# Two more blocks' first product, and block 0's second product, by seven products in a fused retention-and-GELU kernel

## The chip, the cores and the metric

The program runs on one core of one Trainium2 chip. The time is device microseconds of that core, the median of several executions; lower is better. The profile's own "span" (first to last instruction) is about 2 us shorter than the time. All executions quoted here are of the fast state. Ratios are the mean time of one kernel's fast runs over the mean time of the other's fast runs of the same rounds on the same chip, so they are not quite the ratios of the medians that stand beside them.

Engines: PE multiplies matrices and writes the results to a memory called PSUM, which is used in banks; DVE and ACT do element work and empty PSUM; POOL issues most loads here; SP issues stores and DMA transposes. PEld in the profile is PE's loading of the operand that stays in the array during a matmul.

## The reference, cut to what matters

```python
# q, k, v: (8 batches, 8 heads, 576 tokens, 64)
scores = (1/sqrt(64)) * q @ k^T
ret    = scores * where(i >= j, gamma[h] ** (i - j), 0)
x      = (ret @ v), heads side by side            # 4608 x 512
h      = x @ w_in                                 # 512 x 2048
out    = gelu_exact(h) @ w_out                    # 2048 x 512
```

The attention part is done in chunks of 128 tokens (the last of a batch has 64), 40 chunks in all. A chunk's q and k have to be transposed first ("turned" below), on PE or by DMA. The second part is done in 9 blocks of 512 tokens, numbered 0 to 8. Each block has a **first product** (x with w_in, then GELU) and a **second product** (GELU's result g with w_out).

## The kernel before

The program text does not contain a schedule. A builder writes it: it keeps a clock of its own (`clock[0]`), estimates when each operand will be ready, and at each turn emits the next step whose estimate says "ready".

Blocks 1 to 8 already compute the second product by seven products of quarter matrices instead of eight (the Strassen-Winograd scheme): 112 matmuls of 256 columns instead of 64 of 512. `left` is a quarter of g or a sum S1 to S4 of quarters, `right` a quarter of w_out (B) or a sum T1 to T4. Block 0 computes it plainly, in `mlp2_step`.

```python
def mlp_ready(step):                          # "2": block 0, plain
    ...
    if kind == "s":
        return fast_ready(t, step[2])
    ts, m0, m1 = step[2:]
    when = max(land_out[(m1 - 1) // 2],       # <- when this piece of w_out lands
               g_ready(t, ts * 128, ts * 128 + 128, range(m0, m1)))
    ...

def fast_ready(t, n):                         # "s": blocks 1 to 8, seven products
    k, p = (LAST_ORDER if t == N_BLK - 1 else FAST_ORDER)[n]
    lhs, rhs, where = PRODUCTS[k]
    if lhs[0] == "S":
        when = max(s_end.get((t, q_, int(lhs[1])), 1e6) for q_ in range(N_DF // 4))
    else:
        ...
        when = g_ready(t, lo, lo + 128, range(int(lhs[2]) - 1, N_DF, 2))
    ...                                       # accumulators, a free PSUM bank
    if rhs[0] == "T":
        when = max(when, w_sum_end[0])
    return when                               # nothing here asks when w_out ("B") lands
```

## Time and profile before

| | before |
|---|---|
| time | 298.81 us (298.47 to 299.09, 4 runs) |
| span | 296.9 us |
| first `hT` matmul / last matmul starts | 12.5 / 293.1 us |
| PE, DVE, ACT busy | 97%, 57%, 44% |
| granted PE clock | 0.998 |

From the page of the kernel before: the span, the busy time of the engines, and two rows of the span in 40 slices (7.4 us each): busy tenths of PE and granted PE clock in tenths.

```profile
span 296.9 us, 7431 instructions
...
PE 288.6 (97%) x3151; PEld 192.8 (65%) x3151; DVE 169.1 (57%) x368; ACT 130.9 (44%) x259; POOL 113.8 (38%) x146
...
PE   6999999999999999999999999999999999999995
...
PEclk9999999999999999999999999999999999999999
```

PE is full from the second slice on. The clock row has a 9 everywhere, but its record only begins at 15.9 us: matmuls of 128 columns start 107 ns apart at 12.7 us and 55 ns apart at 16.1 us, so the early ones ran at half clock. From 16 us on the clock is full. PE's chain of waits (shares of the span by engine, then by line) also shows PE as the limit:

```profile
PE 84%; DMA 7%; DVE 6%; POOL 2%; issue 1%; POOLq 0%; DVEq 0%
PE hT L403 38%; PE fast L535 32%; DMA v_ld<-in_v_dram 4%; PE sc L295 3%; PE o_ps L331 3%; PE o_ps L370 2%; PE oT L435 2%; PE u_ps L351 2%; DMA w_in<-in_moe_w_in_dram 2%; DMA qk_ld<-in_q_dram 1%; PE qk_ps L270 1%; DVE vh L316 1%; POOL qk_ld L185 1%; DVE s L468 1%; DVE qkT L273 1%
```

`hT` is the first product, `fast` the second by seven products, `oT` the plain one of block 0. Pieces of that chain in order of time (start us, duration us, what):

```profile
113.21 0.24 PE u_ps L351 x8
...
118.01 0.12 PE u_ps L351 x8
...
267.34 13.81 PE hT L403 x64
281.15 12.24 PE fast L535 x112
```

A plain first product of a block lasts 13.81 us, a second product by seven 12.24 us. A group of eight `u_ps` matmuls lasts 0.12 us behind another of its shape and 0.24 us behind another shape, so a change of shape costs about 0.12 us.

### The profile page before, as it was taken

What the parts mean: (1) busy time and instruction counts of PE and PEld (TensorE: products, weight loads), DVE (VectorE), ACT (ScalarE), POOL (GpSimd) and SP (SyncE); (2) the same over time, 40 slices, a digit from 0 to 9 for tenths busy, and PEclk for the clock granted to TensorE, in tenths of its full rate; (3) what the DMA queues carried; (4) which work ended last, traced back from release to release, by engine and by line L of the source; (5) the groups of instructions that cost most, each with busy time, mean ns of one, the idle gap of its engine ahead of it and who ended that gap; (6) DMA issues with size and microseconds to landing.
All of it is one profiled execution on the core that took longest, in us unless ns stands there. A gap on an engine that the chain in (4) does not pass through costs nothing.

```text
span 296.9 us, 7431 instructions
## 1 busy us (share of the span) xinstructions
PE 288.6 (97%) x3151; PEld 192.8 (65%) x3151; DVE 169.1 (57%) x368; ACT 130.9 (44%) x259; POOL 113.8 (38%) x146
## 2 busy tenths in 40 slices
PE   6999999999999999999999999999999999999995
PEld 2675755658865488557864786568656864784584
DVE  4652646947779726986089827581775144402422
ACT  4676502655235613554246414651465146426621
POOL 8997879838485260690781075000000000000000
PEclk9999999999999999999999999999999999999999
DMA  9999999999999999999999999900300030003013
GB/s 92 152 182 176 190 187 187 199 144 131 155 147 202 166 155 149 210 157 166 77 230 137 134 78 223 162 10 3 141 2 2 0 143 0 2 5 137 3 35 106
DMA packets 153089, 35.48 MB, mean 119 GB/s; under 512 B 141792, under 2 KB 148960, under 8 KB 153056
## 3 DMA queue, kind: packets, MB, share of 16 engines
q0 software_dynamic: 117872, 18.23, 86.4%
q1 hardware_dynamic: 35184, 16.78, 31.9%
q8 instruction: 24, 0.39, 0.5%
q14 instruction: 9, 0.07, 0.1%
HBM read 36.70 MB, written 9.44 MB: 155 GB/s over the span
## 4 chain that ended last, share of the span: by engine, by line
PE 84%; DMA 7%; DVE 6%; POOL 2%; issue 1%; POOLq 0%; DVEq 0%
PE hT L403 38%; PE fast L535 32%; DMA v_ld<-in_v_dram 4%; PE sc L295 3%; PE o_ps L331 3%; PE o_ps L370 2%; PE oT L435 2%; PE u_ps L351 2%; DMA w_in<-in_moe_w_in_dram 2%; DMA qk_ld<-in_q_dram 1%; PE qk_ps L270 1%; DVE vh L316 1%; POOL qk_ld L185 1%; DVE s L468 1%; DVE qkT L273 1%
## 5 line engine op out<-in xcount | busy, mean ns | idle before, releaser
L403 PE MATMUL hT<-xT,w_in 128*128 128x512 bf16 (+7 forms) x692 | 130.2, 345 | 1.0 <-DVE xT L382 0.8
L409 ACT ACTIVATE g<-hT 128x512 bf16<-128x512 f32 (+6 forms) x173 | 89.5, 527 | 53.7 <-PE hT L403 50.9
L403 PEld LDWEIGHTS <-w_in 128*128 128x128 bf16 x692 | 62.0, 98 | 59.5 <-issue 0.9
L535 PEld LDWEIGHTS <-s 128*128 128x128 bf16 x512 | 49.6, 98 | 7.0 <-DVE s L468 0.8
L185 POOL DMA_DIRECT2D qk_ld<-in_q_dram x39 | 33.9, 869 | 47.1 <-DMA qkT<-qk_ld 39.9
L306 DVE TENSOR_TENSOR ret<-sc,msk 128x512 bf16<-128x512 f32 x64 | 41.1, 682 | 11.1 <-PE sc L295 10.7
L535 PE MATMUL fast<-w_sum,s 128*128 128x256 bf16 x384 | 43.8, 273 | 0.5 <-DVE s L468 0.5
L535 PEld LDWEIGHTS <-g 128*128 128x128 bf16 x384 | 37.5, 98 | 5.8
L185 POOL DMA_DIRECT2D v_ld<-in_v_dram x39 | 34.0, 871 | 12.9 <-DVE s L468 3.5
L559 DVE TENSOR_TENSOR o_sb<-fast,u 128x512 f32<-128x512 f32 (+1 forms) x18 | 11.4, 631 | 48.2 <-PE fast L535 39.2
L185 POOL DMA_DIRECT2D qk_ld<-in_k_dram x39 | 33.9, 869 | 5.6 <-DMA v_ld<-in_v_dram 4.4
L535 PE MATMUL fast<-w_out,g 128*128 128x256 bf16 x256 | 29.3, 273 | 0.0
L382 DVE TENSOR_TENSOR xT<-o_ps,dq 128x512 bf16<-128x512 f32 (+1 forms) x42 | 24.3, 605 | 7.4 <-PE o_ps L370 5.8
L467 DVE TENSOR_TENSOR s<-g 128x512 bf16<-128x512 bf16 x32 | 13.4, 420 | 25.0 <-ACT g L409 24.8
L555 ACT COPY u<-fast 128x512 f32<-128x512 f32 (+1 forms) x18 | 9.7, 538 | 39.9 <-PE fast L535 39.9
L356 ACT CAST u_sb<-u_ps 128x256 bf16<-128x256 f32 x32 | 11.9, 372 | 32.2 <-PE u_ps L351 32.1
L316 DVE TENSOR_TENSOR vh<-v_ld,dv 128x512 bf16<-128x512 bf16 x32 | 21.2, 680 | 6.4 <-DMA v_ld<-in_v_dram 6.4
L535 PE MATMUL fast<-w_out,s 128*128 128x256 bf16 x128 | 15.6, 272 | 0.0
L535 PE MATMUL fast<-w_sum,g 128*128 128x256 bf16 x128 | 15.3, 273 | 0.0
L435 PE MATMUL oT<-w_out,g 128*128 128x512 bf16 x64 | 15.2, 380 | 0.0
L295 PE MATMUL sc<-qkT 64*64 64x128 bf16 (+1 forms) x576 | 14.1, 223 | 0.5 <-ACT qkT L276 0.4
L468 DVE TENSOR_TENSOR s<-s,g 128x512 bf16<-128x512 bf16 x32 | 13.6, 425 | 1.1
(62 smaller groups left out, 192.6 us busy)
## 6 DMA issues: line engine op xcount, KB each, us to landing
out_dram<-o_sb SPq DMA_DIRECT2D x14, 512.0 KB, 4.7
qk_ld<-in_k_dram POOLq DMA_DIRECT2D x32, 128.0 KB, 7.3
v_ld<-in_v_dram POOLq DMA_DIRECT2D x32, 128.0 KB, 7.4
qk_ld<-in_q_dram POOLq DMA_DIRECT2D x31, 128.0 KB, 7.3
w_in<-in_moe_w_in_dram POOLq DMA_DIRECT2D x8, 256.0 KB, 6.8
w_out<-in_moe_w_out_dram POOLq DMA_DIRECT2D x8, 256.0 KB, 7.8
out_dram<-o_sb SPq DMA_DIRECT2D x4, 256.0 KB, 5.8
out_dram<-o_sb SPq DMA_DIRECT2D x8, 128.0 KB, 1.7
```

The lines of the kernel that those rows point to most:

```text
L185: nc.gpsimd.dma_start(dst[:cs], src[b, :, c0:c0 + cs, :].rearrange("h s d -> s h d"))
L295: nc.tensor.matmul(sc[e][lo:lo + 64, hp, :cs], lhsT=qkT[sl, 1, hp, lo:lo + 64], rhs=qkT[sl, 0, hp, :cs], start=True, stop=True, skip_group ...
L306: nc.vector.tensor_tensor(r[:cs, :, :cs], sc[e][:cs, :, :cs], msk[:cs, :, :cs].to_broadcast([cs, HP, cs]), op=ALU.mult)
L316: nc.vector.tensor_tensor(vh[:cs], loaded[i][1][:cs], dv[:cs, :, ci:ci + 1].to_broadcast([cs, H, D]), op=ALU.mult)
L356: nc.scalar.copy(u, u_ps[0])
L382: nc.vector.tensor_tensor(xT[:, :, at:at + hi - lo], s["o_ps"][:, :, lo:hi], dq[:, :, c0 + lo:c0 + hi], op=ALU.mult)
L403: nc.tensor.matmul(hT[:, :hi - lo], lhsT=w[:, cc, o:o + 128], rhs=xT[:, cc, tok0 % RING + lo:tok0 % RING + hi], start=(cc == 0), stop=(cc ...
L409: nc.scalar.activation(g_of(t, m, lo, hi), hT[:, :hi - lo], AF.Gelu)
L435: nc.tensor.matmul(oT, lhsT=g_of(t, m, ts * 128, (ts + 1) * 128), rhs=w_out_sb[:, m // 2, m % 2, :], start=(m == 0), stop=(m == N_DF - 1))
L467: nc.vector.tensor_tensor(u[:, 0], a[2, 1], a[2, 2], op=ALU.add)
L468: nc.vector.tensor_tensor(u[:, 1], u[:, 0], a[1, 1], op=ALU.subtract)
L535: nc.tensor.matmul(acc_[:, p, :], lhsT=left(t, lhs, j, p), rhs=right(rhs, j), start=(fresh and j == 0 and (p == 0 or apart)), stop=(j == N ...
```

## The change

Its intent: (1) the first product of blocks 7 and 8 also by seven products ("lean"), woven into the second product of the block in front; (2) the second product of block 0 by seven products as well, so that `mlp2_step` goes; (3) the running state sum kept in SBUF instead of in a PSUM bank of its own; (4) attention groups by a list instead of by a rule; (5) another order of the first loads and a finer estimate of DMA times in the builder. The diff, cut to its core:

```diff
-    N_PE_TR = 10
+    N_PE_TR = 9
+    N_DYN = 3
+    N_LEAN = 7
+    LOADS = "1 2 3 i i i 4 i o i i 5 i i 6 o 7 o 8 o o o o o"   # chunks, w_in, w_out
+    PLAN = [(1, 16), (1, 5), (1, 110), (0, 103), ... ]              # 34 groups: chunks, not before
-    FAST_FROM = 1
+    FAST_FROM = 0
...
-    for what in "1 i 2 i i 3 z i i i i i 4 5 o o o o 6 o o o o 7 8".split():
+    for what in LOADS.split():
...
-    def mlp2_step(t, ts, m0, m1):
-        wait(land_out[(m1 - 1) // 2])
-        ...
+    def states(upto):                      # two chunks' states in one bank
+        ...                                # run_sum (SBUF) += u_ps on DVE, u = run_sum on ACT
+    def lean_step(t, n, x):
+        ...                                # 7 products, 4 matmuls of 256 columns each
+        if k == 1: keep("m1")
+        elif k == 2: add("c11", "m1", acc_)
+        ...                                # then GELU from SBUF
...
+    stages = [first_runs[0], first_runs[1] + [second_run[0]], ...]
+        if t + 1 >= N_LEAN and t + 1 < N_BLK:
+            stages.append(lean_runs + [second_run[t]] if LEAN_FIRST else ...)
...
-        if kind == "s":
-            return fast_ready(t, step[2])
-        ts, m0, m1 = step[2:]
-        when = max(land_out[(m1 - 1) // 2], g_ready(t, ts * 128, ts * 128 + 128, range(m0, m1)))
-        return max(when, free_at[first_free()[0]]) if m0 == 0 else when
+        if kind == "f":
+            return lean_ready(*step[1:])
+        return fast_ready(t, step[2])
```

## The prediction

> What bounds the kernel now. The page gives PE 97% busy, DVE 57%, ACT 44%. The chain of waits is 84% PE; from 12.5 us, where the first hT matmul starts, to the last matmul at 293.1 us it is almost only PE. The PE waits list barely 3 us, most of it before 12.5 us. So the span is 12.5 us of start, 280.6 us of PE instructions back to back, and 3.8 us of tail. In the timeline the first product of a late block (64 matmuls of 512 columns) lasts 13.81 us (216 ns each); the second by seven products (112 of 256) lasts 12.23 us (109 ns each). Block 0's second product is still plain: 64 oT matmuls, 13.8 us.
>
> What the change does to PE.
> 1. Blocks 7 and 8: first product by seven products, 4 x 7 x 4 = 112 matmuls of 256 columns: 12.23 instead of 13.81 us, -1.6 us each, -3.2 us.
> 2. Block 0's second product by seven products too (the threshold goes from 1 to 0): -1.6 us.
> 3. Nine instead of ten chunks turned on PE: -0.45 us.
> 4. Listed groups and states of two chunks in one bank. A u_ps group takes 0.12 us behind another of its tile shape and 0.24 us behind another shape (chain): a change of shape costs about 0.12 us. The Trainium skill ("TensorEngine Tiling (Array Packing)", Key Properties) says that changing the mode drains the engine; the trace agrees. I count 107 changes now, and expect 95 to 100 after: -1 us.
> 5. Loads reordered: chunks 1 to 3 ahead of the first w_in piece. The first hT slips from 12.5 to about 16 to 18 us, but then runs 512 wide with more attention behind it; I book 0, with +-2 us. Early matmuls run at 107 ns per 128 columns until 16 us, as the skill's "TensorE: Matmul & The Clock Gate" (Part 1) has it for a cold array; that stays.
> Sum: about -6.3 us.
>
> What it adds elsewhere. DVE: 32 state sums (about 0.4 us each, 13 us), 24 adds of the lean products (0.69 us), about half of 24 copies, sums of w_in (32) and x (8), 16 sums of block 0: 169 to about 220 us. ACT stays near 130 to 140 us. In a woven stage (12.2 + 12.2 us of PE) I count about 21 us of DVE: tight, but two open chains and the second product as filler should cover waits of 0.9 us. The sums of block 8's g can only begin when block 7's use of the sum buffers ends; 16 sums of about 0.35 us against about 5.3 us of PE work that needs none: perhaps 0.3 us of stall. I book +0.5 us for this.
>
> Predicted: 292.5 us, range 289.0 to 296.0; faster by over 2% (below 293.03) 0.57, within 2% 0.41, slower 0.02.
>
> Right or wrong would show as: 224 lean matmuls at 109 ns; hT 512-wide count down by 128; no oT; PE still the chain to the end; two woven stages of about 24.5 us; last stage still about 12.2 us and tail 3.8 us; DVE 215 to 225 us; attention finished some 40 us earlier than the 242 us of now; the first hT later.
>
> What would make it wrong: PE waiting on DVE s, m1/u2/u4 or lean sums in the woven stages (then 294 to 297); early starvation, because all w_out and their sums must land before block 0's second product, while transposes share the DMA (slower); or the listed order removing hidden start stalls, worth 2 to 3 us more than I book (then 289 to 290).

## More of the kernel before

The order in which steps are emitted is the order in each engine's queue. Semaphores keep the result right whatever the order; the estimates decide only the order.

```python
while True:                                   # the builder's loop
    picks = attention_picks()                 # attention, sums, turns of chunks
    due = [p for p in picks if p[0] <= clock[0] + SOON]
    if due: attend(*due[0][1:]); continue
    pick = mlp_pick()                         # a step of a first or second product
    if pick is not None and pick[0] <= clock[0] + SOON:
        mlp(pick[1]); continue
    ...                                       # else move the clock on
```

How block 0 got over the time in which w_out was still landing is to be seen in PE's timeline (start, duration, instruction; no bracket at the end means no idle time before it) and in one stretch of time (its bounds, its length, PE busy, PEld, DVE, ACT, POOL busy, each with its count, then granted clock as a share of full clock, DMA busy share, GB/s):

```profile
35.48 3.63 PE L435 MATMUL oT<-w_out,g 128*128 128x512 bf16 x16
...
52.04 1.04 PE L435 MATMUL oT<-w_out,g 128*128 128x512 bf16 x4
```

```profile
36.00:49.00 13.00, 13.00 (x122) 6.46 (x120) 5.23 (x11) 2.05 (x5) 9.81 (x12) 1.00 1.94 175
```

The plain `oT` takes w_out two rows of tiles at a time, from 35.5 us on, as its pieces land; PE is busy 13.00 of 13.00 us between 36 and 49 us.

## The result, and the profile after

306.50 us (305.60 to 306.76, 4 runs) against 298.81 us; the ratio is 1.0253, 95% interval 1.0227 to 1.0278. The change made the kernel 2.5% slower. Forecast were 292.5 us and at most 296.0.

The page after, same lines as before:

```profile
span 303.9 us, 7902 instructions
...
PE 282.8 (93%) x3304; PEld 209.5 (69%) x3322; DVE 216.6 (71%) x492; ACT 137.2 (45%) x274; POOL 112.5 (37%) x143
...
PE   6889716999999999999999999999999999999995
...
PEclk9999955999999999999999999999999999999999
```

PE's busy time is 5.8 us less than before (288.6 to 282.8), yet the span is 7 us longer. In slices 5 to 7 (30 to 53 us) PE's row has a hole, 7 1 6, and in slices 6 and 7 the granted clock is 5 tenths. The chain of waits has lost PE's share and gained DMA's, with a new name in it:

```profile
PE 80%; DMA 10%; POOL 5%; DVE 2%; issue 1%; POOLq 0%; DVEq 0%
PE fast L573 36%; PE hT L469 28%; PE lean L706 7%; DMA w_out<-in_moe_w_out_dram 5%; DMA w_in<-in_moe_w_in_dram 5%; PE sc L330 3%; PE o_ps L366 2%; POOL qk_ld L224 2%; PE o_ps L422 2%; PE u_ps L389 2%; POOL v_ld L224 1%; POOL w_in L235 1%; DVE u L721 1%; DVE ret L341 0%; POOL qk_ld L113 0%
```

The waits of PE (engine, line, releaser: total us, times, longest us), the new one and that of the lean products:

```profile
PE fast L573 <- DMA w_out<-in_moe_w_out_dram: 10.6, 6, 3.6
...
PE lean L706 <- DVE u L721: 0.5, 1, 0.5
```

PE's timeline at that place (the bracket is idle time before the instruction and its releaser):

```profile
35.06 1.03 PE L469 MATMUL hT<-xT,w_in 128*128 128x512 bf16 x4
35.93 0.44 PE L573 MATMUL fast<-w_out,g 128*128 128x256 bf16 x2
39.93 0.37 PE L573 MATMUL fast<-w_out,g 128*128 128x256 bf16 x1 [3.56 <-DMA w_out<-in_moe_w_out_dram]
43.76 0.37 PE L573 MATMUL fast<-w_out,g 128*128 128x256 bf16 x1 [3.45 <-DMA w_out<-in_moe_w_out_dram]
...
48.88 0.37 PE L573 MATMUL fast<-w_out,g 128*128 128x256 bf16 x1 [0.90 <-DMA w_out<-in_moe_w_out_dram]
49.05 3.41 PE L469 MATMUL hT<-xT,w_in 128*128 128x192 bf16 x20
...
52.84 1.15 PE L469 MATMUL hT<-xT,w_in 128*128 128x192 bf16 x12
```

This is one step, the first of block 0's second product: eight matmuls, one for each piece of w_out. It was emitted at 35.93 us, right behind the last matmul of block 0's first product, and its last matmul started at 48.88 us, when the last piece had landed. Nothing else ran on PE in those 13 us, although 20 matmuls of 192 columns of block 1 stood behind it. The Trainium skill ("PSUM — Partial Sum Buffer", Engine vs sequencer instructions) says that matmuls start and complete in program order; the trace agrees. That stretch, to be held against the one of before, and the next 11 us:

```profile
36.00:49.00 13.00, 2.36 (x9) 0.75 (x8) 3.15 (x8) 0.85 (x2) 9.56 (x13) 0.61 1.72 184
49.00:60.00 11.00, 11.00 (x141) 10.29 (x140) 5.45 (x11) 6.27 (x18) 9.93 (x12) 0.84 2.38 158
```

PE was busy for 2.36 of 13.00 us, and the granted clock fell to 0.61; it was 0.84 in the stretch after. The skill ("TensorE: Matmul & The Clock Gate", Part 1) says that the array's clock falls to half after an idle window of about 3.4 us and needs about as long at work to come back. The trace agrees on the way back: the clock record is full again at 52.5 us, 3.5 us after the work resumed; the twenty matmuls of 192 columns from 49.05 us start 160 ns apart, those from 52.84 us 82 ns apart. On the way down less idle time was enough: the clock fell at 38.9 us, and in the 3.4 us before that PE had been busy for 0.89 us, so idle for 2.5.

```profile
35.48:38.89 3.41, 0.89 (x5) 0.39 (x4) 3.38 (x10) 0.90 (x2) 3.08 (x5) 1.00 2.02 170
38.89:42.31 3.42, 0.37 (x1) 0.10 (x1) 0.29 (x1) 0.00 (x0) 2.39 (x5) 0.50 2.04 172
```

Why it was emitted there: after the change block 0 goes through `fast_ready`, and that asks for g, for sums and for a bank, but not for w_out. For blocks 1 to 8 that had never mattered, because w_out lands once and was there long before. The line that asked, `land_out[...]`, stood in the branch that the change took out. The builder, run once more with a print in it, shows the moment: at 35.07 us of its clock block 1's next piece of x was estimated 0.4 us away, this step was "ready", and so it was put in front. The builder's own estimate for the last piece of w_out was 48.7 us, within 0.2 us of the truth; nobody asked for it. By its clock this order even ends 0.6 us earlier (286.7 us) than the mended one of e1 (287.3 us), so the builder could not have warned.

To see where time went over the whole run I summed, over each trace, the times from the start of one PE matmul to the start of the next, by the kind of the first (us; a wait is counted with the matmul before it):

| kind | before | after | e1 (below) | e9 (below) |
|---|---|---|---|---|
| first products (`hT`, `lean`) | 127.0 | 125.6 | 124.9 | 122.8 |
| second products (`fast`, `oT`) | 113.8 | 123.4 | 112.6 | 111.1 |
| attention (`sc`, `o_ps`, `u_ps`) | 37.8 | 36.3 | 36.4 | 34.6 |
| turns of chunks (`qk_ps`) | 6.1 | 5.8 | 5.4 | 7.6 |
| dummy matmuls and the rest at the start | 7.2 | 8.2 | 8.6 | 7.5 |
| sum | 291.9 | 299.3 | 287.9 | 283.6 |

The second product should have lost 1.6 us and gained 9.6; everything else stands near or below where it stood.

### The profile page after: what moved, and what is told of

It reads as the page before. It is cut to its first block, busy times and chain, and to the rows that moved or that the text cites. A ratio compares the mean times of both kernels' runs of the same rounds, so it can differ in the third digit from the quotient of the medians.

```text
span 303.9 us, 7902 instructions
## 1 busy us (share of the span) xinstructions
PE 282.8 (93%) x3304; PEld 209.5 (69%) x3322; DVE 216.6 (71%) x492; ACT 137.2 (45%) x274; POOL 112.5 (37%) x143
## 4 chain that ended last, share of the span: by engine, by line
PE 80%; DMA 10%; POOL 5%; DVE 2%; issue 1%; POOLq 0%; DVEq 0%
PE fast L573 36%; PE hT L469 28%; PE lean L706 7%; DMA w_out<-in_moe_w_out_dram 5%; DMA w_in<-in_moe_w_in_dram 5%; PE sc L330 3%; PE o_ps L366 2%; POOL qk_ld L224 2%; PE o_ps L422 2%; PE u_ps L389 2%; POOL v_ld L224 1%; POOL w_in L235 1%; DVE u L721 1%; DVE ret L341 0%; POOL qk_ld L113 0%
## 5 line engine op out<-in xcount | busy, mean ns | idle before, releaser
L469 PE MATMUL hT<-xT,w_in 128*128 128x512 bf16 (+6 forms) x576 | 102.1, 330 | 2.1 <-DMA w_in<-in_moe_w_in_dram 1.0
L473 ACT ACTIVATE g<-hT 128x512 bf16<-128x512 f32 (+6 forms) x148 | 71.6, 494 | 65.6 <-PE hT L469 64.1
L469 PEld LDWEIGHTS <-w_in 128*128 128x128 bf16 x592 | 53.9, 100 | 43.9 <-DMA w_in<-in_moe_w_in_dram 1.4
L573 PEld LDWEIGHTS <-s 128*128 128x128 bf16 x576 | 55.8, 98 | 6.9
L573 PEld LDWEIGHTS <-g 128*128 128x128 bf16 x432 | 41.8, 98 | 16.9 <-issue 11.0
L573 PE MATMUL fast<-w_sum,s 128*128 128x256 bf16 x432 | 49.8, 273 | 0.0
L573 PE MATMUL fast<-w_out,g 128*128 128x256 bf16 x288 | 35.4, 275 | 10.6 <-DMA w_out<-in_moe_w_out_dram 10.6
L505 DVE TENSOR_TENSOR s<-g 128x512 bf16<-128x512 bf16 x36 | 15.1, 419 | 12.6 <-ACT g L473 11.6
L404 ACT CAST u_sb<-run_sum 128x256 bf16<-128x256 f32 x24 | 9.7, 405 | 21.3 <-DVE run_sum L401 14.9
L308 DVE COPY qkT<-qk_ps 128x512 bf16<-128x512 bf16 (+1 forms) x12 | 4.3, 396 | 19.2 <-PE qk_ps L305 19.2
L507 DVE TENSOR_TENSOR s<-g 128x512 bf16<-128x512 bf16 x36 | 15.0, 418 | 0.0
## 6 DMA issues: line engine op xcount, KB each, us to landing
qk_ld<-in_k_dram POOLq DMA_DIRECT2D x32, 128.0 KB, 7.0
v_ld<-in_v_dram POOLq DMA_DIRECT2D x32, 128.0 KB, 7.1
qk_ld<-in_q_dram POOLq DMA_DIRECT2D x31, 128.0 KB, 7.2
out_dram<-o_sb SPq DMA_DIRECT2D x8, 128.0 KB, 1.7
```

The lines of the kernel that those rows point to most:

```text
L469: nc.tensor.matmul(hT[:, :hi - lo], lhsT=w[:, cc, o:o + 128], rhs=xT[:, cc, tok0 % RING + lo:tok0 % RING + hi], start=(cc == 0), stop=(cc ...
L473: nc.scalar.activation(g_of(t, m, lo, hi), hT[:, :hi - lo], AF.Gelu)
L505: nc.vector.tensor_tensor(u[:, 0], a[2, 1], a[2, 2], op=ALU.add)
L507: nc.vector.tensor_tensor(u[:, 2], a[1, 1], a[2, 1], op=ALU.subtract)
L573: nc.tensor.matmul(acc_[:, p, :], lhsT=left(t, lhs, j, p), rhs=right(rhs, j), start=(fresh and j == 0 and (p == 0 or apart)), stop=(j == N ...
```

## The experiments

Theory A: the one step emitted 13 us too early caused the loss, by holding PE and then by the cold clock; the rest of the change works. Rival B: w_out lands late because the DMA queues are full, and PE starves then in whatever order. Rival C: the woven stages and the added DVE work (216.6 against 169.1 us busy) cost the time. All kernels gave correct results. The times of e1, e2, e3, e6, e7 and e10 fell where theory A or the prediction's view put them; those of e4, e8, e9 and e11 missed their forecasts, as told below.

### e1: only the readiness rule mended

```diff
+        if rhs[0] == "B":
+            when = max(when, max(land_out))
         if rhs[0] == "T":
             when = max([when] + list(w_sum_end.values()))
```

> The changed kernel with one thing mended: the readiness rule of the second product also waits for all w_out pieces, so block 0's first step is listed after block 1's first matmuls instead of at 35.9 us. Theory A (one step of 8 matmuls, placed in PE's queue 13 us before its operands land, held up all that stood behind it): the waits of fast on w_out (10.6 us) go and so does the cold array after them; 306.5 falls to 294 to 297. Rival B (w_out lands late because the DMA queues are full, so PE starves then whatever the order): 302 or more. Rival C (the woven stages or the extra DVE work cost the time): 304 to 306.

Measured: 294.46 us (294.24 to 295.80) against 298.83 us of before on that chip, ratio 0.986 (0.981 to 0.991): clear of noise. Against the 306.50 us of the changed kernel two lines give back 12.0 us. (The changed kernel ran in another call; the kernel before has the same median in both, 298.81 and 298.83 us, so the medians may be compared.) Slices, timeline and stretches of e1, as shown of the others:

```profile
PE   6979999999989999999999999999999999999995
...
PEclk9999999999999999999999999999999999999999
```

```profile
37.02 2.15 PE L469 MATMUL hT<-xT,w_in 128*128 128x192 bf16 x24 [0.43 <-DVE xT L434]
...
56.26 3.66 PE L575 MATMUL fast<-w_out,g 128*128 128x256 bf16 x32
```

```profile
36.00:49.00 13.00, 11.88 (x221) 10.27 (x220) 12.71 (x28) 7.88 (x23) 9.54 (x13) 1.00 1.71 184
49.00:60.00 11.00, 11.00 (x99) 8.82 (x98) 6.88 (x11) 7.00 (x18) 9.34 (x12) 1.00 2.48 157
```

The step now starts at 56.26 us behind block 1's first product, the clock stays at 1.00, and the waits of `fast` on w_out are gone from the list. The DMA queues are as busy as in the changed kernel in that stretch (184 GB/s in both), so rival B falls: PE had other work, and the order kept it from it.

### e2 and e3: without the lean first products, with and without the mend

```diff
-    N_LEAN = 7
+    N_LEAN = 9
```

> The changed kernel with the early stall kept, but blocks 7 and 8 computed with the plain first product (the threshold raised to 9). Theory A: the lean products are worth their matmul saving of 3.2 us, so this runs at about 309 to 310. Rival C: they cost time, so this runs below 306.

> Both edits: the mended readiness rule and no lean first products. Theory A: the two effects add, so about 3 us above e1_landing. Rival C: at or below e1_landing.

Measured: e2 309.44 us (308.68 to 309.90), 2.9 us above the changed kernel; e3 298.10 us (296.14 to 298.66), 3.6 us above e1, both on the chip of e1. The lean products are worth what their matmuls save (3.2 us was forecast), stall or no stall. Rival C falls. The chain of e1 shows that the woven stages have no hole worth naming:

```profile
227.53 1.75 PE lean L708 x16
...
269.26 20.18 PE fast L575 x184
289.47 0.42 DVE o_sb L599
```

From 227.53 us to the last element work at 289.47 us PE does five things of 12.23 us each (two lean first products, the second products of blocks 6, 7 and 8), 61.2 us in 61.9 us. DVE's extra work is off the path there. e3 is also the change without its main idea, and it is no faster than the kernel before (0.9955, 0.990 to 1.001): what else it brought came to nearly nothing.

### e4: the stall kept, but the array kept at work

```diff
         for j in range(N_DF // 2):
+            if t == 0 and n == 0:
+                warm((0, 0, 14, 14, 4, 4, 4, 4)[j])      # dummy matmuls of 512 columns
             nc.tensor.matmul(acc_[:, p, :], ...)
```

> The changed kernel, stall kept, but dummy matmuls put between the eight waiting matmuls of the step, fewer than fit the waits, so that the array has work while it waits. It splits theory A's loss in stall and cold clock after it. The hT matmuls of 192 columns just behind the stall took about 160 ns instead of 83 ns, some 6 us at half rate: 2.5 to 3.5 us should be won, 303 to 304. If the clock plays no part: 306.5, the same.

Measured: 304.35 us (304.23 to 305.10), 2.2 us below the changed kernel, somewhat less than forecast. So of the 12.0 us that e1 gives back, about 2.2 us were the cold clock after the stall and the remaining 9.9 us or so the stall itself (306.50 - 304.35, and 304.35 - 294.46). The forecast took 6 us at half rate; the trace of the changed kernel has 3.5 us of work at half rate (49.05 to 52.54 us), half of which, 1.75 us, is an estimate of the same loss. The split is good to about half a microsecond. Part of the timeline, and the stretch:

```profile
41.03 0.27 PE L575 MATMUL fast<-w_out,g 128*128 128x256 bf16 x1
41.25 3.18 PE L891 MATMUL warm<-zeros 128*128 128x512 bf16 x14
44.27 0.27 PE L575 MATMUL fast<-w_out,g 128*128 128x256 bf16 x1
...
49.46 1.81 PE L469 MATMUL hT<-xT,w_in 128*128 128x192 bf16 x20
```

```profile
36.00:49.00 13.00, 12.77 (x79) 6.22 (x80) 4.98 (x13) 1.50 (x3) 9.54 (x13) 1.00 1.72 184
```

The matmuls of 192 columns behind the stall now start 82 ns apart from the first on (20 in 1.65 us). The stretch is also a warning. The skill's "Perfetto Trace Analysis" (Identifying the Most-Contended Engine) calls matmul busy time a bad measure of how close a kernel is to its limit, because matmuls are pipelined; here it misleads for another reason: PE is busy 12.77 of 13.00 us, 10.4 us of it with dummies. A gap can be hidden from the busy share as well as filled.

### e6: e1 with block 0's second product plain again

`mlp2_step` and its readiness rule put back for block 0 (`FAST_FROM = 1`), all else as in e1.

> e1_landing with block 0's second product plain again, as in the kernel before (64 matmuls of 512 columns that take the w_out pieces two by two as they land), all else as in e1_landing. Prediction's view: the seven products are worth 1.6 us there, so 296.0. Rival: at that time DVE and DMA set the pace (16 sums of g are 5.9 us of DVE between 28 and 37 us, and every w_out piece must have landed), so the saving is lost: within 0.5 us of e1_landing (294.5) or below it.

Measured: 296.13 us (295.71 to 299.88) against 299.50 us of before on that chip, ratio 0.992 (0.982 to 1.002); e1 had 0.986 on another chip. The difference of the ratios, 0.006, is 1.8 us (one of e6's four runs, 299.88 us, raises its mean); by medians, each against its own before, it is 1.0 us; between the profiled spans it is 1.5 us (294.0 and 292.5). PE's time on second products, summed as in the table above, is 114.1 us in e6 and 112.6 us in e1, also 1.5 us. The intervals overlap, so the size is uncertain, but 1.0 to 1.8 us fits the forecast 1.6 us and speaks against the rival that DVE and DMA eat the saving.

### e7: rule as it was, w_out loaded earlier

```diff
-    LOADS = "1 2 3 i i i 4 i o i i 5 i i 6 o 7 o 8 o o o o o"
+    LOADS = "1 2 3 i i i 4 i i i i i 5 o o o o o o o o 6 7 8"
```

> The changed kernel with its readiness rule as it was, and only the order of the first loads changed: all w_in pieces, chunk 5, all eight w_out pieces, then chunks 6 to 8. The early step stays early (the kernel's own bookkeeping places it at 33 us), but its operands should land at about 42 us instead of 48.9. Theory A: the waits of fast on w_out shrink from 10.6 us to 5 to 8 us; but x of block 1 comes later, so PE has less to do after it, and little of that is won in the total: 302 to 307. If the place of the step were not the cause but the lateness of w_out alone, it should come near e1_landing (294.5).

Measured: 306.24 us (305.05 to 307.47) against 299.82 us of before on that chip, ratio 1.022 (1.018 to 1.026); the changed kernel has 1.025. The waits on w_out halved, and others came in their place:

```profile
PE fast L573 <- DMA w_out<-in_moe_w_out_dram: 5.1, 6, 1.0
PE o_ps L366 <- DVE ret L341: 2.7, 6, 0.7
...
PE fast L573 <- DVE w_sum L490: 0.9, 1, 0.9
```

The step stalled less, but chunks 6 to 8 now came behind w_out, and PE waited for attention's operands (`ret`) more than before, 2.7 us against 0.7; that the order of the chunks is the reason was not tested. The clock took a part too. It fell at 39.2 us although no wait on w_out was longer than 1.02 us; PE had been busy for 0.81 of the 3.4 us before:

```profile
35.75:39.17 3.42, 0.81 (x3) 0.29 (x3) 3.26 (x10) 0.00 (x0) 2.21 (x4) 1.00 1.24 205
39.17:42.58 3.41, 1.68 (x8) 1.02 (x8) 0.00 (x0) 0.00 (x0) 2.45 (x4) 0.50 2.10 166
```

After the stall PE worked for about 7.4 us at half clock (41.3 to 46.0 and 50.1 to 52.8 us), against 3.5 us in the changed kernel; half of the difference, 2 us, is an estimate of what that cost more. Moving data to suit a wrong order did not help; moving the instruction did.

### e8, e9, e10, e11: new lists under the mended rule

`LOADS` and `PLAN` look like the result of a search by the builder's clock, which then held the faulty rule. I searched both lists anew by random changes under the mended rule, by the builder's own clock, and ran two results. Against e1 only the two lists differ; e9's are:

```diff
-    LOADS = "1 2 3 i i i 4 i o i i 5 i i 6 o 7 o 8 o o o o o"
+    LOADS = "i 1 2 3 i i 4 i 5 i 6 i i i 7 8 o o o o o o o o"
-    PLAN = [(1, 16), (1, 5), (1, 110), (0, 103), ... ]
+    PLAN = [(1, 136), (0, 119), (1, 187), (0, 100), (1, 94), (1, 22), (1, 0), (0, 184), (2, 175), (0, 103), (1, 9),
+            (1, 0), (0, 14), (2, 24), (1, 51), (2, 61), (2, 15), (1, 16), (2, 0), (2, 15), (2, 31), (2, 20), (2, 0),
+            (2, 3), (2, 96), (2, 102), (2, 47), (2, 174), (1, 30), (2, 35), (0, 150), (0, 174), (0, 24), (0, 60)]
```

> e1_landing with the order of the first loads and the list of attention groups searched anew under the mended readiness rule; nothing else changes. The bookkeeping gains 2.5 us over e1_landing, most of it at the start. If the list had been fitted to the faulty rule, the chip shows 1.5 to 3 us: 291.5 to 293. If the bookkeeping has no more to give on the chip: 294 to 295.

> As e8_fix_retuned, another result of the same search, with all w_out pieces last. Bookkeeping 2.4 us below e1_landing. 291.5 to 293 if the new lists hold on the chip, with the eight w_out pieces landing last and no wait of fast on them.

Measured on one chip (before: 299.82 us): e8 294.28 us (292.81 to 294.69), ratio 0.982 (0.977 to 0.986), no more than 0.2 us below e1 by the medians and 1.3 us by the ratios (0.0045 of 299 us), a miss; e9 290.32 us (289.99 to 293.78), ratio 0.972 (0.966 to 0.978). e9 is 2.8% faster than the kernel before and beats both kernels of this case, and its own forecast (291.5 to 293). The builder's clock had put e8 0.1 us ahead of e9; the chip put it 4 us behind by the medians, 2.9 by the ratios. What the estimate leaves out that tells them apart I did not settle. e9's first `hT` and its first `fast`, and its three longest waits of PE:

```profile
11.42 0.61 PE L469 MATMUL hT<-xT,w_in 128*128 128x128 bf16 x8
...
54.55 3.66 PE L575 MATMUL fast<-w_out,g 128*128 128x256 bf16 x32
```

```profile
PE row_ps L158 <- DVE diag L149: 1.3, 1, 1.3
PE warm L155 <- DVE zeros L91: 1.3, 1, 1.3
PE o_ps L366 <- DVE vh L351: 1.0, 1, 1.0
```

A w_in piece loaded first lets the first `hT` start at 11.42 us, where e1 has 18.1 us, and no wait of PE after that exceeds 1.0 us. In the table above e9 is 2.1 us below e1 in first products, 1.5 in second products, 1.8 in attention and 1.1 in dummies, and 2.2 us above it in turns.

The last call puts the old rule back into e9, and runs e9 again beside it:

> e9_fix_retuned_b with only the mended rule taken out again: new lists, old rule. The bookkeeping now lists four steps of block 0's second product at 36 us, and thinks itself 0.6 us slower than e9 by that. Theory A: PE stands before them until the last w_out piece has landed at 49 us, 9 to 13 us of waits of fast on w_out, and the time goes to 299 to 305. Rival (the new lists, not the rule, brought the gain): within 2 us of e9 (290 to 292.5).

> e9_fix_retuned_b once more, unchanged, on the chip of e10, so that the two stand side by side and the best time is seen twice: 290 to 291.

Measured: e10 304.18 us (303.86 to 305.09), e11 291.16 us (289.92 to 291.66), before 299.58 us; ratios 1.016 and 0.971 (e11's 291.16 lies 0.2 us above its forecast). The rule alone is worth 13.0 us under these lists, 12.0 us under those of the change. The stretch of e10:

```profile
36.00:49.00 13.00, 3.80 (x14) 1.16 (x12) 3.77 (x10) 0.82 (x2) 8.43 (x12) 0.63 1.49 194
```

PE was busy 3.80 of 13.00 us at a granted clock of 0.63, the hole of the changed kernel again; e9 has 12.95 of 13.00 us there. One thing differs from the expectation, 9 to 13 us of waits on w_out: the profile puts down 6.3 us to w_out, and the 2.9 us before the step's first matmul to a sum on DVE that this step does not read. What that first wait was for stays open. The builder thought this order 0.6 us slower than e9's; it was 13.

## Why the prediction was wrong

Its step 2, "Block 0's second product by seven products too (the threshold goes from 1 to 0): -1.6 us", failed. The saving in matmuls was about right (e6), but the step took for granted that the new path would be listed only when its operands were there. It was listed 13 us before, because the readiness rule of that path never asked for w_out. The prediction did name the danger ("early starvation, because all w_out and their sums must land before block 0's second product"), gave "slower" 0.02, and looked for it in transposes and DMA. It could have been found without a run: the diff removes the only lines that asked when a w_out piece itself lands before a step is listed, and the load order puts five of eight w_out pieces last. (The 292.5 us is 298.8 less 6.3; the 0.5 us that the prediction books for DVE is not in it.)

| term | forecast | measured |
|---|---|---|
| lean first products, blocks 7 and 8 | -3.2 us | -3.6 (e3 to e1), -2.9 (e2 to the change) |
| block 0's second product, matmuls | -1.6 | about -1.0 to -1.8 (e6 to e1), uncertain; -1.5 by sums by kind |
| its place in the queue | not seen | +12.0 (change to e1): stall about 9.9, cold clock about 2.2 |
| one chunk fewer turned on PE | -0.45 | -0.7 in e1 (sums by kind) |
| groups and states listed | -1 | -1.4 in attention in e1 (sums by kind); changes of shape 107 to 86 |
| loads reordered, start | 0, +-2 | first `hT` 12.5 to 17.8 us; dummies +1.4 in e1 |
| total without the stall | -6.3, +0.5 for DVE | -4.4 (e1) |

Without the start the measured terms sum to about -7.2 us (-3.6, -1.5, -0.7, -1.4), and e1 gained 4.4. Most of the missing 2.8 us is on the side of the start (these figures mix medians and sums over single traces, so they are good to some tenths): e3, which has the plain first products of before, spends 128.0 us on them where the kernel before spends 127.0, probably because three blocks instead of two are taken in narrow pieces as x arrives (argued, not tested); with 1.4 us more of dummies that makes about 2.4 us, which the prediction had booked as 0. e9 shows that it need not be lost.

Of the other signs that the prediction named: 224 lean matmuls at 109 ns (right), DVE 215 to 225 us (216.6, right), no `oT` (right), woven stages of about 24.5 us (right), the first `hT` at 16 to 18 us (17.8, right). That early matmuls stay at half clock until 16 us was wrong for the new orders: e9's first `hT` matmuls, at 11.4 us, start 55 ns apart. The 512-wide `hT` count fell by 184, not 128, since block 2 goes in narrow pieces too. Attention ended at 228.5 us in the changed kernel and 217 us in e1, not 40 us before 242. The feared stalls on DVE sums in the woven stages are 0.5 us, once.

## What to carry to other kernels

When a step is sent through another path, compare the two paths' readiness rules, not only their costs: a condition that was always true for the old users of a path may be false for the new one. On an engine that works in program order a step listed too early costs not its own length but the time until its last operand lands (here 0.9 us of work cost 12.0 us), and semaphores keep the result right, so only the trace tells. When an estimate is mended, lists that were chosen under it are worth a new search, and several of the results should be run, since the estimate ranked two of them wrongly by 3 to 4 us.

## What the Trainium skill lacked or had wrong

- "PSUM — Partial Sum Buffer", Engine vs sequencer instructions, has the program order of matmuls, but neither it nor "Perfetto Trace Analysis" (Sequencer Loop), where an instruction waits for its semaphores, puts the consequence in numbers: eight matmuls waiting for DMA held all PE work behind them for 13 us, and 12.0 us of that came back when they were listed later.
- "TensorE: Matmul & The Clock Gate" (specifications) says that the queue pulls weight loads ahead of matmuls in flight. Of a matmul that waits for a semaphore it says nothing. The trace shows one load ahead, that of the waiting matmul itself (started at 36.1 us for the matmul at 39.9 us); the first load of the work behind the step started at 48.88 us, together with the step's last matmul.
- The same page's Part 1 held on the way back: 3.5 us of work at half clock. For the way down its table asks for an idle window of about 3.4 us, and the page knows of short idle times that have the same effect, without saying how many it takes. Here the clock fell after 3.4 us in which PE was idle for 2.5 us (changed kernel) or 2.6 us (e7, in waits of at most 1.02 us).
- "TensorEngine Tiling (Array Packing)", Key Properties, says that a change of mode drains the array, without a time; here it was about 0.12 us.
- "Perfetto Trace Analysis" (Identifying the Most-Contended Engine) warns of matmul busy time because of pipelining. Dummies are a second reason: e4 was 98% busy in a stretch of 13.0 us of which 10.4 us were dummies.
